# One-bank row tiles for the two seven-row output units of a soft-MoE kernel

## The chip, the cores and the metric

The kernel runs on one core of one Trainium2 chip. The metric is the device time of one execution in microseconds, the median of several runs. Lower is better.

## The reference

Four sequences of 5056 tokens with 256 channels go through a gated recurrence. The result goes, as one list of 20224 tokens, through a mixture of 8 experts with 4 slots each. Cut to what matters:

```python
h = f[:, t] * h + i[:, t] * x[:, t]          # recurrence over t; y[:, t] = h
logits = x @ phi                             # x is now y, as 20224 x 256; phi 256 x 32
d = exp(logits - logits.max(0)); d /= d.sum(0)
slot_input = d.T @ x                         # 32 x 256
slot_out = relu(slot_input[e] @ w1[e]) @ w2[e]   # 4 slots of each expert e
c = exp(logits - logits.max(1)); c /= c.sum(1)
out = c @ slot_out                           # 20224 x 256, float32, 20.7 MB
```

Only the last line is touched by the change: each token's output is a weighted sum of 32 slot rows, divided by the sum of its weights.

## The kernel before

Up to about 143 us the kernel runs the recurrence, the logits and the experts. It keeps three things for the end. `etall` holds exp(logits) as [slot, token], with the 32 slots of batch b on partitions 32b to 32b+31. `rrow` holds the reciprocal of each token's sum of weights. `slot_out` holds the slots' outputs on 128 partitions, a copy for each batch, and `slot_bd` (line 685, written by POOL) is the same in a block form, two batches side by side: with the weights of two batches on 64 partitions, one matmul against `slot_bd` gives 512 columns, 256 of each batch.

The 5056 tokens of a batch are cut into `blocks`: two of 2048 tokens (16 rows of 128), a last one of 896 (7 rows), and 64 tokens left over. A row is 128 tokens, one on each partition; within a block a partition holds consecutive tokens, so that a transfer writes 16 KB (or 7 KB) in one piece. The output stage works through units, in this order, written out by hand:

1. `pieces(0, 0)` (line 712): block 0 of batch 0 in nine small pieces, a matmul for each row, so that the first transfers can start early. Its PSUM tiles come from `pfirst`, eight buffers of one bank.
2. `couple(2, 0)` and `couple(2, 1)` (line 742): the seven-row block for batches 0 and 1, then for batches 2 and 3. Each tile of `pout` has two banks and takes two rows of two batches, so a unit has four tiles, the last with one row.
3. `rest()` (line 768): the 64 left-over tokens of all batches.
4. `whole(0, 1)` (line 731): block 0 of batch 1, four rows to a tile.
5. `couple(0, 1)`, `couple(1, 0)`, `couple(1, 1)`: sixteen rows of two batches each, eight tiles.

In every unit PE writes a PSUM tile, and DVE and ACT take the tiles in turn: they multiply by `rrow` into an SBUF tile (`ob` or `oc` of the pool `osb`, three buffers each). When a unit is complete, SP issues its transfers to HBM: 7 for `pieces`, two for each couple (one a batch), two for `rest`, one for `whole`, 20 in all. They go through one queue in the order of issue. Order on each engine is that of the program (a manual schedule).

A PSUM tile is reused when its reader has finished. A pool that opens where another one lay waits for all of the earlier pool's tiles: `pfirst` and `pout` both cover all eight banks, and `pout` opens behind `pieces`. Later tiles of `pout` wait only for the one whose buffer they take: `rest` for a tile of `couple(2, 1)` that DVE reads, `whole`'s first for one that ACT reads.

```python
with tc.tile_pool(name="pfirst", bufs=8, space=PSUM) as pfirst:
    pieces(0, 0)

pout = ctx.enter_context(tc.tile_pool(name="pout", bufs=4, space=PSUM))
```

Of the kernel before, what the change touches and what calls it, by code (L numbers as in the profile page):

```python
# [9 lines left out]
F32 = mybir.dt.float32  # L10
# [3 lines left out]
ACT = mybir.ActivationFunctionType  # L14
# [4 lines left out]
def kernel(  # L19
# [10 lines left out]
    nc = tc.nc  # L30
    B, S, D = x.shape
    E = moe_w1.shape[0]
    F = moe_w1.shape[2]
    NS = moe_phi.shape[1]
    SPE = NS // E
    P = 128
# [25 lines left out]
    blocks = [(i * P * wide_r, wide_r) for i in range(n_blk)]  # L62
# [57 lines left out]
    etall = store.tile([P, S + PAD], BF16, name="etall")[:, :S]  # L120
    rrow = store.tile([P, n_grp * R, B], F32, name="rrow")
# [6 lines left out]
    slot_bd = store.tile([P, 2, D], BF16, name="slot_bd")  # L128
# [33 lines left out]
    with tc.tile_pool(name="sp2", bufs=3) as sp2, \  # L162
# [316 lines left out]
        for n in range(n_unit):  # L479
# [14 lines left out]
            else:  # L494
                end = n >= n_unit - 6
# [94 lines left out]
        for o in range(DC):  # L590
            nc.tensor.matmul(sin_ps[:, o], slot_v[:, o], rep[:, 0],
                             start=True, stop=True, skip_group_check=True)
        spin(slot_bank[:, 1], 6, D)

    with tc.tile_pool(name="ew", bufs=1) as ew, \
# [16 lines left out]
        for q in range(E // Q):  # L612
            hi = ew.tile([P, F], BF16, name=f"hi{q}")
            for k in range(2):
                hi_ps = (psu.tile([P, H], F32, name="hi_ps", tag="up") if q == 0 else
                         pbig.tile([P, H], F32, name="hi_ps", tag=f"hi_ps{k}"))
                for o in range(DC):
                    for j in range(Q):
                        nc.tensor.matmul(hi_ps[ds(j * NS, NS)], sin[:, o],
                                         w1_sb[q * Q + j][:, o, ds(k * H, H)],  # L620
                                         start=(o == 0), stop=(o == DC - 1),
                                         skip_group_check=True)
# [30 lines left out]
        for e in range(Q):  # L653
            for fc in range(FC):
                nc.tensor.matmul(so4_ps[ds(fc % 4 * NS, NS), :], hid[:, fc, e],
                                 w2_sb[e][:, fc],
                                 start=(e == 0 and fc < 4),
                                 stop=(e == Q - 1 and fc >= FC - 4),
                                 skip_group_check=True)
# [7 lines left out]
        for j in range(Q):  # L667
            for fc in range(FC):
                nc.tensor.matmul(so_ps, wide[:, fc, j].rearrange("p b s -> p (b s)"),
                                 w2_sb[Q + j][:, fc], start=j == 0 and fc == 0,  # L670
                                 stop=j == Q - 1 and fc == FC - 1, skip_group_check=True)
            if j == 0:
                nc.tensor.matmul(so_ps, rep2, so4, start=False, stop=False,
                                 skip_group_check=True)
# [14 lines left out]
    with tc.tile_pool(name="osb", bufs=3) as osb:  # L689

        def by_vector(ob, op, scale):
            nc.vector.tensor_tensor(ob, op, scale.broadcast_to(list(ob.shape)), ALU.mult)  # L692
# [5 lines left out]
        def share(op, i, b, r, k):  # L698
            t0, n_r = blocks[i]
            ew = etall[ds(b * NS, NS), ds(t0, P * n_r)].rearrange("s (p r) -> s p r", r=n_r)  # L700
            for j in range(k):
                nc.tensor.matmul(op[:, j], ew[:, :, r + j], slot_out[ds(b * NS, NS)],  # L702
                                 start=True, stop=True, skip_group_check=True)

        def scale_of(i, b, r, k):
            return rrow[:, ds(blocks[i][0] // P + r, k), ds(b, 1)]

        def rows_of(i, b):
            t0, n_r = blocks[i]
            return out[ds(b * S + t0, P * n_r)].rearrange("(p r) d -> p r d", r=n_r)  # L710

        def pieces(i, b):
            dst = rows_of(i, b)
            obs = [osb.tile([P, blocks[i][1], D], F32, name="ob", tag="ob") for _ in range(2)]
            for j, r, k, ready in ((0, 0, 1, 1), (1, 1, 1, 1), (0, 2, 2, 2), (1, 4, 2, 2),
                                   (0, 6, 2, 2), (1, 8, 2, 0), (0, 12, 2, 0), (1, 10, 2, 4),
                                   (0, 14, 2, 4)):
                op = pfirst.tile([P, 2, D], F32, name="op", tag="op")
                share(op, i, b, r, k)
                (by_vector, by_scalar)[j](obs[j][:, ds(r, k)], op[:, ds(0, k)],  # L720
                                          scale_of(i, b, r, k))
                if ready:
                    q = ds(r + k - ready, ready)
                    nc.sync.dma_start(out=dst[:, q], in_=obs[j][:, q])

        with tc.tile_pool(name="pfirst", bufs=8, space=PSUM) as pfirst:
            pieces(0, 0)

        pout = ctx.enter_context(tc.tile_pool(name="pout", bufs=4, space=PSUM))

# [11 lines left out]
        def couple(i, j):  # L742
            t0, n_r = blocks[i]
            ew = etall[ds(j * 2 * NS, 2 * NS), ds(t0, P * n_r)].rearrange(
                "s (p r) -> s p r", r=n_r)
            scale = rrow[:, ds(t0 // P, n_r), ds(2 * j, 2)]
            ob = osb.tile([P, 2, n_r, D], F32, name="oc", tag="oc")
            for t, r in enumerate(range(0, n_r, 2)):
                k = min(2, n_r - r)
                op = pout.tile([P, 2, 2, D], F32, name="op", tag="op")  # L750
                for i_r in range(k):
                    nc.tensor.matmul(op[:, i_r].rearrange("p u d -> p (u d)"),  # L752
                                     ew[:, :, r + i_r],
                                     slot_bd[ds(j * 2 * NS, 2 * NS)].rearrange("s u d -> s (u d)"),
                                     start=True, stop=True, skip_group_check=True)
                if t % 2 == 0:
                    nc.vector.tensor_tensor(  # L757
                        ob[:, :, ds(r, k)].rearrange("p u r d -> p r u d"), op[:, ds(0, k)],
                        scale[:, ds(r, k)].unsqueeze(3).broadcast_to([P, k, 2, D]), ALU.mult)
                else:  # L760
                    for i_r in range(k):
                        for u in range(2):
                            nc.scalar.activation(ob[:, u, r + i_r], op[:, i_r, u], ACT.Copy,  # L763
                                                 scale=scale[:, r + i_r, ds(u, 1)])
            for u in range(2):
                nc.sync.dma_start(out=rows_of(i, 2 * j + u), in_=ob[:, u])

        def rest():
            n_p = B // 2
            op = pout.tile([P, n_p, 2, D], F32, name="op", tag="op")  # L770
            ob = osb.tile([P, n_p, D], F32, name="ob", tag="ob")
            for j in range(n_p):
                k = ds(j * 2 * NS, 2 * NS)
                nc.tensor.matmul(op[:, j].rearrange("p u d -> p (u d)"),
                                 left[k].rearrange("s t u -> s (t u)"),
                                 slot_bd[k].rearrange("s u d -> s (u d)"),
                                 start=True, stop=True, skip_group_check=True)
            nc.scalar.copy(ob, op[:, :, 0])
            nc.vector.tensor_tensor(ob, ob, op[:, :, 1], ALU.add)
            by_vector(ob, ob, rrow[:, n_grp * R - 1, ds(0, n_p)].unsqueeze(2))  # L780
            dst = out.rearrange("(b t) d -> t b d", b=B)
            for j in range(n_p):
                nc.sync.dma_start(out=dst[ds(S - L, L), ds(2 * j, 2)], in_=ob[:, j])

        end = len(blocks) - 1
        couple(end, 0)
        couple(end, 1)
        rest()
        whole(0, 1)
        for i in range(end):  # L790
# [33 lines left out]
```

## Time and profile before

| what | value |
|---|---|
| three runs | 198.64, 199.23, 199.25 us; median 199.23 |
| the profiled execution | 198.84 us, span 197.1 us |
| busy over the span | PE 77%, DVE 72%, ACT 70%, POOL 52% |
| HBM read, written | 58.23 MB, 20.71 MB |
| first output transfer issued | 144.10 us |
| couple(2, 0), couple(2, 1) issued from | 150.59 and 153.29 us |
| rest, whole(0, 1) issued from | 155.39 and 158.01 us |
| couple(0, 1), (1, 0), (1, 1) issued from | 164.72, 170.80 and 176.87 us |
| SP's last wait, for the output transfers | 17.1 us |

Times within the profile are counted from the start of the span. Busy shares are averages over stages with different limits, so the table says little about the end; the stretches and the timeline from 143 us on do. A busy PE is not PE at its peak, and its clock is granted in steps, which the page shows in tenths. In a timeline line the first number is the start, the second how long the group took, then engine, line, operation, out<-in, shapes and count, and in brackets the idle time before and who ended it. "PEld" is the loading of weights into PE, "SPq" an instruction that SP issues.

### The profile page before, as it was taken

The numbers are of one execution on the slowest core, as the hardware profiler recorded it, in microseconds if no ns is written. First come the engines' busy times: TensorE is split into PE (matmuls) and PEld (weight loads), VectorE is DVE, ScalarE is ACT, GpSimd is POOL, SyncE is SP. The second block draws the span as 40 slices with busy tenths as digits, with TensorE's granted clock in tenths as the row PEclk, the third lists the DMA queues.
The fourth block names the chain that finished last, engine by engine and source line by source line (L and its number), as shares of the span: only waits on it lengthen the run. The fifth ranks groups of instructions, "written<-read, shape, count | busy, mean of one in ns | idle before, by whom it ended". The sixth has DMA issues, their size and how long they took to land.

```text
span 197.1 us, 3226 instructions
## 1 busy us (share of the span) xinstructions
PE 151.9 (77%) x1195; PEld 106.4 (54%) x1195; DVE 142.1 (72%) x163; ACT 138.1 (70%) x193; POOL 103.1 (52%) x78
## 2 busy tenths in 40 slices
PE   0688598897999979897998888999769999960000
PEld 0477478675766758665776676668543643310000
DVE  2669769989799999999999999342268878850000
ACT  3588678799799998899997797240057889990000
POOL 2589578874998588894969977291030000000000
PEclk9999879999999999999999999999985555555555
DMA  5999999999999999999999999999658999999995
GB/s 201 418 420 423 428 431 421 426 427 358 378 429 421 392 353 426 421 412 308 408 419 381 254 220 215 213 214 213 122 197 352 429 429 432 449 429 426 426 426 216
DMA packets 14161, 70.75 MB, mean 359 GB/s; under 512 B 1585, under 2 KB 2866, under 8 KB 10178
## 3 DMA queue, kind: packets, MB, share of 16 engines
q1 hardware_dynamic: 11520, 62.13, 76.1%
q0 software_dynamic: 2624, 8.42, 21.4%
q8 instruction: 9, 0.15, 0.3%
q14 instruction: 6, 0.05, 0.1%
q10 hardware_dynamic: 2, 0.00, 0.0%
HBM read 58.23 MB, written 20.71 MB: 401 GB/s over the span
## 4 chain that ended last, share of the span: by engine, by line
DMA 29%; PE 27%; DVE 17%; POOL 7%; ACT 5%; issue 4%; ACTq 0%; SPq 0%; DVEq 0%; POOLq 0%
DMA x_t<-in_x_dram 14%; DVE h L313 12%; PE op L752 12%; DMA w_sb<-in_moe_w_dram 7%; DMA w_t<-in_moe_w_dram 7%; POOL u_t L246 6%; PE hp L326 3%; PE up L267 3%; DVE ht L345 3%; PE sp L261 2%; PE op L702 2%; PE slot_ps L183 1%; PE lg L359 1%; DVE ob L692 1%; ACT oc L763 1%
## 5 line engine op out<-in xcount | busy, mean ns | idle before, releaser
L246 POOL TENSOR_TENSOR u_t<-s_t,x_t 128x1024 bf16<-128x1024 bf16 (+1 forms) x39 | 82.4, 2129 | 22.1 <-ACT s_t L235 14.3
L313 DVE TENSOR_TENSOR_SCAN h<-a,h,up 128x512 bf16<-128x512 f32 (+1 forms) x72 | 86.8, 1252 | 4.4 <-PE up L267 1.7
L235 ACT ACTIVATE s_t<-f_t 128x2048 bf16<-128x2048 f32 (+2 forms) x23 | 38.3, 1668 | 6.4 <-DMA f_t<-in_f_logit_dram 6.0
L326 PE MATMUL hp<-ident_f,h 128*128 128x128 f32 (+1 forms) x160 | 29.5, 309 | 8.0 <-DVE ht L345 6.0
L326 PEld LDWEIGHTS hp<-ident_f,h 128*128 128x128 f32 (+1 forms) x160 | 23.2, 207 | 19.0 <-DVE ht L345 12.6
L261 PE MATMUL sp<-ident_f,s_t 128*128 128x128 f32 x144 | 22.3, 300 | 6.4 <-ACT s_t L235 4.5
L752 PE MATMUL op<-slot_bd,etall 64*128 64x512 bf16 x62 | 25.0, 621 | 1.6 <-DVE ob L692 1.4
L295 ACT ACTIVATE a<-sp,lbs 128x1024 f32<-128x1024 bf16 x24 | 25.4, 1115 | 0.6 <-PE sp L261 0.6
L763 ACT ACTIVATE oc<-op,rrow 128x256 f32<-128x256 f32 x60 | 22.7, 488 | 3.6 <-PE op L752 3.0
L757 DVE TENSOR_TENSOR oc<-op,rrow 128x1024 f32<-128x1024 f32 x16 | 19.3, 1222 | 6.0 <-PE op L752 6.0
L261 PEld LDWEIGHTS sp<-ident_f,s_t 128*128 128x128 f32 x144 | 18.0, 155 | 8.4 <-ACT s_t L235 5.4
L302 ACT ACTIVATE a<-sp,lbs 128x512 f32<-128x512 bf16 (+2 forms) x22 | 17.8, 858 | 4.7 <-PE sp L261 4.3
L267 PE MATMUL up<-ident_f,u_t 64*128 64x64 f32 x192 | 17.8, 230 | 2.2 <-POOL u_t L246 2.1
L752 PEld LDWEIGHTS <-etall 64*128 64x128 bf16 x62 | 9.0, 155 | 16.1 <-issue 12.5
L267 PEld LDWEIGHTS up<-ident_f,u_t 64*128 64x128 f32 x192 | 14.0, 138 | 6.2 <-POOL u_t L246 2.8
L183 PE MATMUL slot_ps<-rep,ident_f 128*128 128x256 f32 x52 | 16.7, 417 | 0.0
L345 ACT COPY ht<-hp 128x512 f32<-128x512 f32 (+1 forms) x20 | 11.6, 582 | 3.8 <-PE hp L326 3.7
L345 DVE COPY ht<-hp 128x512 f32<-128x512 f32 (+1 forms) x20 | 13.3, 666 | 0.8 <-PE hp L326 0.8
L696 ACT ACTIVATE ob<-op,rrow 128x256 f32<-128x256 f32 x15 | 5.8, 477 | 11.2 <-PE op L702 11.1
L313 DVE TENSOR_TENSOR_SCAN h<-a,up 128x512 bf16<-128x512 f32 x8 | 9.3, 1208 | 2.6 <-ACT a L302 1.7
L261 PE MATMUL up<-ident_f,u_t 128*128 128x128 f32 x48 | 9.5, 328 | 0.7 <-POOL u_t L246 0.7
L359 PE MATMUL lg<-h,phi 128*32 128x512 bf16 (+1 forms) x80 | 9.4, 389 | 0.3 <-ACT et L383 0.2
(110 smaller groups left out, 147.9 us busy)
## 6 DMA issues: line engine op xcount, KB each, us to landing
f_t<-in_f_logit_dram SPq DMA_DIRECT2D x12, 1024.0 KB, 12.3
x_t<-in_x_dram SPq DMA_DIRECT2D x12, 1024.0 KB, 11.9
out_dram<-oc SPq DMA_DIRECT2D x6, 2048.0 KB, 11.1
w_sb<-in_moe_w_dram POOLq DMA_DIRECT2D x14, 512.0 KB, 10.9
f_t<-in_f_logit_dram SPq DMA_DIRECT2D x12, 512.0 KB, 8.5
x_t<-in_x_dram SPq DMA_DIRECT2D x12, 512.0 KB, 9.9
out_dram<-oc SPq DMA_DIRECT2D x4, 896.0 KB, 5.2
out_dram<-ob SPq DMA_DIRECT2D x1, 2048.0 KB, 8.3
```

The costliest lines, as they stand in the source:

```text
L183: nc.tensor.matmul(slot_bank[:, 1], ident_f, wide_rep, start=False, stop=False, skip_group_check=True)
L235: nc.scalar.activation(s_t, f_t, ACT.Sigmoid, scale=-1.0)
L246: nc.gpsimd.tensor_tensor(uts[n][:, :r], s_t[:, :r], x_t[:, :r], ALU.mult)
L261: nc.tensor.transpose(ps[:, :, r], t[:, r], ident_f)
L267: nc.tensor.transpose(v[:, :, r], t(r)[k].bitcast(F32), ident_f[k, k])
L295: nc.scalar.activation(a, sp[:, :, :, :, o], ACT.Identity, scale=nomlb[:, ds(o, 1)], bias=1.0)
L313: nc.vector.tensor_tensor_scan(h[:, :T, o], decays[n // 2, o][:, n % 2, :T], up[:, :T, o], hs[number(g - 1, b)][:, ds(used(g - 1) - 1, 1), ...
L326: nc.tensor.transpose(hp[:n_p, r], hw[:, :n_p, r], ident_f)
L345: copy(hts[g][:n_p, b].rearrange("p r d -> p (r d)").bitcast(F32), hps.pop(n)[:n_p].rearrange("p r c -> p (r c)"))
L752: nc.tensor.matmul(op[:, i_r].rearrange("p u d -> p (u d)"), ew[:, :, r + i_r], slot_bd[ds(j * 2 * NS, 2 * NS)].rearrange("s u d -> s (u d)"),
L757: nc.vector.tensor_tensor(ob[:, :, ds(r, k)].rearrange("p u r d -> p r u d"), op[:, ds(0, k)], scale[:, ds(r, k)].unsqueeze(3).broadcast_t ...
L763: nc.scalar.activation(ob[:, u, r + i_r], op[:, i_r, u], ACT.Copy, scale=scale[:, r + i_r, ds(u, 1)])
```

## The change

The two seven-row units leave `couple` and get a function of their own, `by_rows`. It takes one tile of one bank for each row, with both batches in it (512 columns), from `pfirst`, in turn with the pieces' tiles. Even rows (four of seven) are evicted by DVE in one instruction of 512 columns; odd rows (three) by ACT in two of 256, one a batch. Matmuls, their order, the SBUF tile and the two transfers stay as they were. `pout` opens behind `by_rows`, so its first user is now `rest`.

```diff
+        def by_rows(i, j):
+            t0, n_r = blocks[i]
+            k = ds(j * 2 * NS, 2 * NS)
+            ew = etall[k, ds(t0, P * n_r)].rearrange("s (p r) -> s p r", r=n_r)
+            scale = rrow[:, ds(t0 // P, n_r), ds(2 * j, 2)]
+            ob = osb.tile([P, 2, n_r, D], F32, name="oc", tag="oc")
+            for r in range(n_r):
+                op = pfirst.tile([P, 2, D], F32, name="op", tag="op")
+                nc.tensor.matmul(op.rearrange("p u d -> p (u d)"), ew[:, :, r],
+                                 slot_bd[k].rearrange("s u d -> s (u d)"),
+                                 start=True, stop=True, skip_group_check=True)
+                if r % 2 == 0:
+                    by_vector(ob[:, :, r], op, scale[:, r].unsqueeze(2))
+                else:
+                    for u in range(2):
+                        nc.scalar.activation(ob[:, u, r], op[:, u], ACT.Copy,
+                                             scale=scale[:, r, ds(u, 1)])
+            for u in range(2):
+                nc.sync.dma_start(out=rows_of(i, 2 * j + u), in_=ob[:, u])
+
+        end = len(blocks) - 1
         with tc.tile_pool(name="pfirst", bufs=8, space=PSUM) as pfirst:
             pieces(0, 0)
+            by_rows(end, 0)
+            by_rows(end, 1)
 
         pout = ctx.enter_context(tc.tile_pool(name="pout", bufs=4, space=PSUM))
...
-        end = len(blocks) - 1
-        couple(end, 0)
-        couple(end, 1)
         rest()
         whole(0, 1)
```

On the engines' queues the number of matmuls, weight loads, activations and transfers is unchanged. DVE has eight instructions of 512 columns in place of four of 1024 (the last of each four with 512). In the second unit each row waits for the eviction of a row of the first unit, and the first matmul of `rest` waits for the last evictions of DVE and of ACT; `whole`'s first three tiles carry no wait of their own any more.

## The prediction

> **What bounds the kernel now.** I read the slices of the page first, then the stretches of the output stage with their transfer rates, then the timeline there, then the issues and landings. The slices (40 of 4.93 us) say who works last:
>
> ```profile
> PE   0688598897999979897998888999769999960000
> ...
> ACT  3588678799799998899997797240057889990000
> ...
> PEclk9999879999999999999999999999985555555555
> DMA  5999999999999999999999999999658999999995
> ```
>
> From about 152 us on DMA is at 9 and goes on for four slices after PE and ACT have stopped. So the end is set by output transfers. They run in one queue, in order of issue, and the stretches (columns: busy us and instruction count of PE, PEld, DVE, ACT, POOL; granted clock; DMA share; GB/s) show where that queue was not fed:
>
> ```profile
> 143.00:146.10 3.10, 1.97 (x16) 1.74 (x16) 2.62 (x6) 2.45 (x7) 1.83 (x2) 1.00 0.29 95
> 146.10:150.50 4.40, 3.81 (x11) 1.36 (x12) 2.70 (x4) 2.25 (x7) 0.00 (x0) 0.50 1.04 416
> 150.50:151.50 1.00, 1.00 (x4) 0.51 (x4) 1.00 (x2) 0.63 (x2) 0.00 (x0) 0.50 0.20 80
> 151.50:156.30 4.80, 4.80 (x21) 2.63 (x17) 3.69 (x5) 3.98 (x11) 0.00 (x0) 0.50 1.01 423
> 156.30:165.60 9.30, 9.30 (x25) 3.62 (x25) 7.56 (x8) 8.38 (x22) 0.00 (x0) 0.50 1.01 423
> ```
>
> There is one hole once the stream runs: in 150.5 to 151.5 the share is 0.20, so 0.8 us are lost. The timeline has its cause:
>
> ```profile
> 143.12 1.97 PE L702 MATMUL op<-slot_out,etall 32*128 32x256 bf16 x16
> 143.25 1.83 POOL L685 TENSOR_SCALAR slot_bd<-slot_out,parity 128x256 bf16<-128x256 bf16 x2 [9.64 <-DVE slot_out L683]
> 143.55 2.81 DVE L692 TENSOR_TENSOR ob<-op,rrow 128x256 f32<-128x256 f32 x5 [0.48 <-PE op L702]
> 143.65 2.68 ACT L696 ACTIVATE ob<-op,rrow 128x256 f32<-128x256 f32 x7 [10.28 <-PE op L702]
> ...
> 146.51 3.41 PE L752 MATMUL op<-slot_bd,etall 64*128 64x512 bf16 x9 [1.42 <-DVE ob L692]
> ...
> 147.63 1.22 DVE L757 TENSOR_TENSOR oc<-op,rrow 128x1024 f32<-128x1024 f32 x1 [1.27 <-PE op L752]
> ...
> 150.59 4.30 SPq L766 DMA_DIRECT2D out_dram<-oc  x4
> ```
>
> PE finishes the pieces at 145.09 and stands for 1.42 us until DVE (146.36) and ACT (146.33) have evicted the last of them: the two-bank pool lies on the banks of the first. DVE then stands 1.27 us for its first tile. So the first seven-row unit is issued at 150.59, when the pieces' bytes have just run out (150.5); its first bytes move some 0.84 us after the issue.
>
> A second margin matters as much. Ahead of couple(0, 1) the queue carries 2.10 MB of pieces, 3.67 of the seven-row units, 0.26 of the rest and 2.10 of whole(0, 1): 8.13 MB. Adding rate times length over the five stretches gives 8.17 MB by 165.6, so the queue runs dry there. couple(0, 1) is issued at 164.72, and with the same 0.84 its bytes start at 165.56. It arrives just in time. A hole filled earlier only pays if this issue moves too. It hangs on PE:
>
> ```profile
> 151.69 0.58 PE L774 MATMUL op<-slot_bd,left 64*128 64x512 bf16 x1
> ...
> 152.76 3.61 PE L702 MATMUL op<-slot_out,etall 32*128 32x256 bf16 x16
> ...
> 156.32 19.28 PE L752 MATMUL op<-slot_bd,etall 64*128 64x512 bf16 x48
> ...
> 164.72 13.79 SPq L766 DMA_DIRECT2D out_dram<-oc  x6
> ```
>
> From whole's first matmul (152.76) to that issue it is 11.96 us of dense PE work.
>
> **The change, part by part.**
>
> *Removed: the pool boundary ahead of unit 0.* Its rows take the eight one-bank buffers in turn. The first seven follow pieces that were evicted between 144.1 and 146.33, each before PE comes to its row. What is left is slot_bd: 143.25 + 1.83 = 145.08, plus 0.05 for a semaphore (slot_out's end at 143.07 to PE at 143.12). PE's first row starts at 145.13 and not at 146.51.
>
> *Replaced: eviction by row.* DVE had two 1024-wide tiles a unit, 1.22 each; now four 512-wide rows. The trace's mean for that shape is 0.68; two of them back to back take 1.28, so they follow at 0.60. Eight rows are 4.8 us against 4 x 1.14 = 4.6 (two 1024-wide in 2.36: 1.14 apart): 0.2 us more DVE work, hidden behind the stream; if the cover goes, 0.2 is its price. ACT keeps its 12 activations at about 0.36. PE keeps 14 matmuls.
>
> [...]
>
> *Unit 0's transfers.* DVE's rows start right behind the pieces, at 146.28; the fourth ends at 146.28 + 3 x 0.60 + 0.68 = 148.76. Before, issue followed DVE's end by 0.08; so 148.84, first bytes 149.7, before the pieces run out at 150.5. The hole of 0.8 us closes.
>
> *Unit 1.* If DVE paces, its last row ends at 146.28 + 7 x 0.60 + 0.68 = 151.16. If PE paces at the granted 0.50 from the start, rows are 0.43 apart (1.86 for four, the last one longer; 48 in 19.28): unit 0's seventh starts at 147.7, unit 1's first almost beside it (it uses the other 64 partitions, as L774 at 151.69 lies 0.07 from the L752 at 151.76), its seventh at 150.3, result 0.63 later, eviction 0.68 and a semaphore: 151.65.
>
> *Added: the boundary now lies ahead of rest.* Its first matmul (L774, 151.69 before) must wait for all fourteen rows: 151.2 to 151.7. Queued behind it on PE are rest's second matmul, whole's sixteen and all 48 of the couples, and on these hang DVE, ACT and SP. But whole no longer waits by itself. Before, it waited until 152.71 for an ACT tile of unit 1 (activations from 151.14); now it follows rest's first matmul by 0.43: 151.6 to 152.1, earlier by 1.1 to 0.6. ACT and DVE reach rest earlier too (ACT was busy to 153.3 with unit 1).
>
> *The transfers moved.* All twenty keep order, size and queue. The first six of unit and rest are issued 0 to 1.8 us earlier, behind a longer backlog, which costs SP time but starves nothing.
>
> *The sum.* The queue before couple(0, 1) runs dry at 165.6 - 0.8 = 164.8. couple(0, 1) is issued at 164.72 - 1.1 to 164.72 - 0.6, its bytes can start at 164.4 to 164.95. So the gain is 0.8 at one end and 0.65 at the other. I take 0.75, nearer DVE's pace, since the first PE rows still run at clock 1.00 (it falls near 146.1). All later transfers (12.6 MB) follow without a gap. The profiled execution took 198.84 (span 197.1 and 1.7 around it): 198.1. The median of the runs, 199.23, lies 0.4 above it: **198.5**.
>
> *The clock.* PE stood idle for about 1 us when the clock fell, and then 19 us of dense 64-partition matmuls did not bring it back. [...]
>
> **The rivals.**
>
> *The hole is smaller in other executions (chance 0.30).* Where the clock falls later than 146.1, PE in the kernel before does unit 0's rows 0.22 apart instead of 0.43 (the pieces' own matmuls were 0.12 apart at 1.00 and whole's 0.22 at 0.50), and unit 0 is issued 0.5 us or more earlier by itself. For it: three runs of the same kernel spread by 0.6 us (198.64 to 199.25), nearly the hole. Against it: two of three lie at the top. The gain is then 0.1 to 0.5: about 198.9.
>
> *The wait ahead of rest takes over (0.13, slower).* The place is rest's first matmul, behind the slowest of fourteen evictions. whole starts later than 152.76 if the last row ends after 152.3, that is if DVE's eight rows take over (152.3 - 146.36) / 8 = 0.74 each. For it: a lone 512-wide row takes 0.68 to 0.69, and two dependent ones on DVE were 0.72 apart. Against it: 0.60 in the pieces, the same operation from the same tiles. Beyond that point every delay is paid in full at couple(0, 1); at 0.80 a row, 0.5 us: 199.7.
>
> *It does not do what it says (0.07).* If PE cannot start before 146 (slot_bd later than POOL's rough span says, or a buffer held), unit 0 gets out at about 150 and rest starts at about 152.5: hole smaller by half, couple(0, 1) no earlier: 199.2. Against it: before, PE's wait named the last evictions, not POOL.
>
> **How the numbers follow.** The forecast has 0.50. About 0.3% (0.6 us) is what a measurement of this kernel can tell from no change; so faster means below 198.63, and the forecast's own range, 198.3 to 198.6, lies just beyond it. The first and third rival are no change, 0.37; the second is slower, 0.13. The range reaches down to 197.9, the lowest run before less 0.75, and up to 199.5, into the slower case.
>
> **What would show it.** Right: PE's first row near 145.1; unit 0 issued near 148.8; no stretch under a share of 0.9 after 146.5; rest's first matmul by 151.7, whole by 152.1; couple(0, 1) issued before 164.1. Wrong: DVE's rows 0.74 or more apart; a new hole where whole(0, 1) ends, near 164.7; or unit 0 issued before 150 in another execution of the old kernel.

## The result

| kernel | median, us | lowest to highest | runs |
|---|---|---|---|
| before | 198.64 | 197.78 to 199.53 | 17 |
| changed | 197.94 | 197.76 to 198.15 | 17 |

The ratio is 0.9968, with a 95% interval of 0.9953 to 0.9983: 0.64 us less, between 0.34 and 0.93. The profiled executions took 198.84 and 198.15 us. Two things stand out. The gain is there, small and clear of noise; and the changed kernel spreads over 0.4 us where the kernel before spreads over 1.75 (a later set of twelve runs of the changed kernel spread further, see "Half of the change"). Their lowest times are the same.

The stretches of the changed kernel's output stage (columns as before: busy us and counts of the five engines, granted clock, DMA share, GB/s):

```profile
146.10:150.50 4.40, 2.99 (x10) 0.98 (x8) 4.40 (x9) 4.40 (x13) 0.00 (x0) 0.71 1.03 409
150.50:151.50 1.00, 0.36 (x2) 0.11 (x2) 0.58 (x1) 0.15 (x1) 0.00 (x0) 0.50 1.06 442
151.50:156.30 4.80, 4.80 (x21) 2.96 (x20) 3.64 (x4) 3.11 (x8) 0.00 (x0) 0.50 1.02 426
156.30:165.60 9.30, 9.30 (x25) 3.46 (x23) 7.25 (x6) 8.50 (x23) 0.00 (x0) 0.50 1.05 440
```

The hole is gone: the share in 150.5 to 151.5 went from 0.20 to 1.06, and no other of these stretches lost anything. DVE and ACT are busy for all of 146.1 to 150.5, where each stood idle before. The timeline of the same kernel:

```profile
145.06 1.69 PE L734 MATMUL op<-slot_bd,etall 64*128 64x512 bf16 x8
146.12 4.52 ACT L741 ACTIVATE oc<-op,rrow 128x256 f32<-128x256 f32 x12
146.22 4.86 DVE L692 TENSOR_TENSOR oc<-op,rrow 128x512 f32<-128x512 f32 x8
147.05 2.48 PE L734 MATMUL op<-slot_bd,etall 64*128 64x512 bf16 x6 [0.30 <-ACT oc L741]
...
148.77 4.00 SPq L744 DMA_DIRECT2D out_dram<-oc  x4
...
151.14 0.60 PE L797 MATMUL op<-slot_bd,left 64*128 64x512 bf16 x2 [1.61 <-DVE oc L692]
...
151.68 3.63 PE L702 MATMUL op<-slot_out,etall 32*128 32x256 bf16 x16
...
155.26 19.30 PE L775 MATMUL op<-slot_bd,etall 64*128 64x512 bf16 x48
...
163.66 13.79 SPq L789 DMA_DIRECT2D out_dram<-oc  x6
```

PE goes from the pieces to the rows without a stop; eight DVE rows take 4.86 us in one run; the first unit is issued at 148.77 and couple(0, 1) at 163.66, 1.8 and 1.1 us earlier than before. PE now waits 1.61 us ahead of rest, until DVE's last row is done; it does no harm, since rest and couple(0, 1) still come earlier than before.

### The profile page after: what moved, and what is told of

Its sections match the earlier page's. It is cut to its first block, busy times and chain, and to the rows that moved or that the text cites. A ratio compares the mean times of both kernels' runs of the same rounds, so it can differ in the third digit from the quotient of the medians.

```text
span 196.4 us, 3226 instructions
## 1 busy us (share of the span) xinstructions
PE 151.1 (77%) x1195; PEld 106.5 (54%) x1195; DVE 142.3 (72%) x167; ACT 138.4 (70%) x193; POOL 103.2 (53%) x78
## 4 chain that ended last, share of the span: by engine, by line
PE 34%; DMA 23%; DVE 18%; POOL 7%; issue 4%; ACT 2%; ACTq 0%; DVEq 0%; POOLq 0%
DVE h L313 11%; PE op L775 10%; DMA w_sb<-in_moe_w_dram 7%; DMA w_t<-in_moe_w_dram 7%; DMA x_t<-in_x_dram 7%; POOL u_t L246 6%; PE hp L326 5%; PE sp L261 5%; PE up L267 4%; DVE ht L345 3%; DVE oc L692 2%; PE slot_ps L183 2%; PE lg L359 2%; DMA f_t<-in_f_logit_dram 2%; PE op L702 2%
## 5 line engine op out<-in xcount | busy, mean ns | idle before, releaser
L775 PE MATMUL op<-slot_bd,etall 64*128 64x512 bf16 x48 | 19.3, 621 | 0.0
L786 ACT ACTIVATE oc<-op,rrow 128x256 f32<-128x256 f32 x48 | 18.2, 492 | 1.1 <-PE op L775 0.5
L780 DVE TENSOR_TENSOR oc<-op,rrow 128x1024 f32<-128x1024 f32 x12 | 14.5, 1223 | 4.3 <-PE op L775 4.3
L183 PE MATMUL slot_ps<-rep,ident_f 128*128 128x256 f32 x52 | 17.5, 432 | 0.0
L775 PEld LDWEIGHTS <-etall 64*128 64x128 bf16 x48 | 7.2, 158 | 11.6 <-issue 10.3
```

What stands on the lines that cost most here:

```text
L183: nc.tensor.matmul(slot_bank[:, 1], ident_f, wide_rep, start=False, stop=False, skip_group_check=True)
L775: nc.tensor.matmul(op[:, i_r].rearrange("p u d -> p (u d)"), ew[:, :, r + i_r], slot_bd[ds(j * 2 * NS, 2 * NS)].rearrange("s u d -> s (u d)"),
```

## The experiments

Times of experiments stand beside runs of the kernel before on the same chip, with medians of 198.72 to 198.82. Places in the output stage are also given from PE's first matmul of the pieces, since that starts at 143.0 to 143.3 us in nearly every execution. "Lost" is the idle time of the 16 DMA engines once the stream was running, averaged over the engines, from the packet records of the trace; it is good to about 0.05 us.

### The kernel before, profiled again

> The kernel before, unchanged, profiled once more. Theory (the granted clock sets the hole): where the clock falls within 0.5 us of 146.1 counted as before, the first seven-row unit is issued near 150.6 and the stream has a hole of about 0.8 us; where it falls after 147.5, that unit is issued at 149.6 to 150.0, the hole is 0.3 us or less and the time is 0.5 us or more lower. Rival (the spread of the times comes from the load stage, ahead of 143 us): the stage from 143 us to the end takes the same 52 us in every execution, and the difference lies before it.

> As for the first look: the same kernel in another execution. Theory: the length from the first matmul of the pieces to the last transfer goes with the time at which the clock falls, 0.8 us between an early and a late fall. Rival: that length is the same, and the start of the output stage moves.

| execution | clock falls, from first matmul | first seven-row unit issued | lost | time, us |
|---|---|---|---|---|
| before, the profile shown | 3.0 | 7.47 | 0.85 | 198.84 |
| before, second profile | 4.9 | 6.53 | 0.18 | 197.98 |
| before, third profile | 4.8 | 6.52 | 0.14 | 198.15 |
| changed | 4.9 | 5.71 | 0 | 198.15 |

From the second profile, two stretches and the timeline:

```profile
146.10:150.40 4.30, 3.65 (x12) 1.65 (x14) 3.45 (x4) 2.55 (x7) 0.00 (x0) 0.72 1.04 417
150.40:150.90 0.50, 0.50 (x3) 0.15 (x1) 0.38 (x1) 0.49 (x2) 0.00 (x0) 0.50 1.06 438
```

```profile
146.53 1.76 PE L752 MATMUL op<-slot_bd,etall 64*128 64x512 bf16 x7 [1.42 <-DVE ob L692]
147.23 3.55 DVE L757 TENSOR_TENSOR oc<-op,rrow 128x1024 f32<-128x1024 f32 x3 [0.85 <-PE op L752]
...
149.67 0.81 SPq L766 DMA_DIRECT2D out_dram<-oc  x2
```

PE waits the same 1.42 us at the boundary. But at full clock seven matmuls take 1.76 us, DVE waits 0.85 and not 1.27, and the unit is issued at 149.67, before the pieces' bytes run out. So the same kernel loses 0.85 us or some 0.15, by where the clock falls; of the 0.15 a part is lost at the first seven-row unit and a part ahead of couple(0, 1), near 164.7 us. The three start the pieces at 143.12 to 143.29 us, so the stage before them does not make this difference. The changed kernel's profile takes as long as the third although it lost nothing: its stream began worse, with a share of 0.53 in the microsecond from 145.3 us against 0.77 in the second profile, before the stretch that "lost" counts. In the three profiles of before the clock falls 3.0, 4.9 and 4.8 us after the same matmul; what sets that moment was not shown.

### PE kept busy at the boundary

```diff
             pieces(0, 0)
+            kept = pfirst.tile([P, 2, D], F32, name="kept", tag="op")
+            for _ in range(5):
+                nc.tensor.matmul(kept.rearrange("p u d -> p (u d)"), ident, etall[:, ds(0, 2 * D)],
+                                 start=True, stop=True, skip_group_check=True)
```

> The kernel before, with five full-array matmuls (128 partitions, 512 columns, 1.1 us at full clock) on PE between the pieces and the pool boundary; nothing reads what they write, the output is the same. Theory (the hole depends on the clock): PE stays at clock 1.00 until 148 us or later in most executions, the first unit's rows come 0.22 apart, it is issued at 149.6 to 150.0, the hole shrinks to 0.3 us or less: 0.3 to 0.7 us faster than the kernel before in the median, and the spread of its times shrinks to under 0.8 us. Rival (the boundary alone makes the hole): no change in the median, 198.4 to 198.9, same spread of 1.7 us.

Measured: 197.98 (197.85 to 198.12, 12 runs) against 198.76 (197.86 to 199.09): ratio 0.9969, 0.9956 to 0.9981. Its timeline:

```profile
145.00 1.25 PE L730 MATMUL kept<-etall,ident 128*128 128x512 bf16 x5
146.49 1.69 PE L756 MATMUL op<-slot_bd,etall 64*128 64x512 bf16 x7 [0.24 <-DVE ob L692]
...
149.63 0.84 SPq L770 DMA_DIRECT2D out_dram<-oc  x2
```

```profile
146.10:150.50 4.40, 3.69 (x14) 1.62 (x15) 3.55 (x4) 2.79 (x8) 0.00 (x0) 0.87 1.04 415
150.50:151.50 1.00, 1.00 (x5) 0.21 (x2) 0.61 (x2) 1.00 (x4) 0.00 (x0) 0.50 1.08 450
```

The boundary, the two-row tiles and the order are those of the kernel before, yet the time and the spread are those of the changed one. The clock fell 6.25 us after the first matmul, and nothing was lost. So in these runs the hole needs two things at once: the wait at the boundary (1.42 us) and a clock that falls early, by about the time the unit's first matmuls run (3.0 us after the first matmul, where 0.85 us were lost, against 4.8 and 4.9, where 0.14 and 0.18 were). Taking away either is worth the same, with ratios of 0.9968 and 0.9969. That the rows need no late fall is seen in two kernels further down that keep the change and have their fall 3.1 us after the first matmul (the one of "The second margin, by itself" and the one with 19 transfers and the pieces as they were): the first unit is issued after 5.72 us in both, as in the changed kernel's profile with its fall at 4.9.

### Rows, but behind the boundary

```diff
             pieces(0, 0)
+        with tc.tile_pool(name="prows", bufs=8, space=PSUM) as prows:
             by_rows(end, 0)
             by_rows(end, 1)
...
-                op = pfirst.tile([P, 2, D], F32, name="op", tag="op")
+                op = prows.tile([P, 2, D], F32, name="op", tag="op")
```

> The change with one part undone: the rows keep one bank and eviction by row, but their eight buffers are a pool of their own that opens behind the pieces, so the boundary is back ahead of the first unit. Theory (the gain is the removed wait at the boundary): PE starts the rows near 146.5 and not 145.1; with the clock at 0.50 the first unit is issued near 150.4 and whole starts 0.7 us later than in the kernel before; with the clock at 1.00 it is issued near 149.5. Median between 198.2 and 199.4, and the spread of the kernel before, over 1 us. Rival (eviction by row is the gain, by letting DVE start on half a tile): near the changed kernel, 197.9 to 198.1, with its small spread of 0.4 us.

Measured: 198.74 (198.06 to 199.18, 12 runs), ratio to before 1.0006, 0.9987 to 1.0024. One stretch and the timeline:

```profile
150.30:151.20 0.90, 0.16 (x1) 0.00 (x0) 0.90 (x2) 0.90 (x4) 0.00 (x0) 1.00 0.20 79
```

```profile
146.43 4.03 PE L734 MATMUL op<-slot_bd,etall 64*128 64x512 bf16 x14 [1.42 <-DVE ob L692]
146.99 0.69 DVE L692 TENSOR_TENSOR oc<-op,rrow 128x512 f32<-128x512 f32 x1 [0.71 <-PE op L734]
...
147.85 0.69 DVE L692 TENSOR_TENSOR oc<-op,rrow 128x512 f32<-128x512 f32 x1 [0.16 <-PE op L734]
...
150.32 3.99 SPq L744 DMA_DIRECT2D out_dram<-oc  x4
```

DVE's first row comes 0.6 us before the first two-row tile of the kernel before, and that gains nothing: at half clock PE paces the rows, DVE waits 0.16 before each, the unit goes out at 150.32 and the hole is back at a share of 0.20. whole starts 9.96 us after the first matmul, 0.3 later than in the kernel before and not 0.7 as expected: the clock came back for a while (last section). The gain of the change is the wait that it removes, not eviction by row.

### Half of the change

```diff
             by_rows(end, 0)
-            by_rows(end, 1)
...
+        couple(end, 1)
         rest()
```

> The changed kernel, unchanged, as the measure for the others here. Every theory: 197.8 to 198.2, spread under 0.5 us.

> Half of the change: the first seven-row unit by rows from the first pool, the second as two-row tiles from the two-bank pool, whose boundary now lies between the two units. Theory (two margins: the hole at 150.5 and the issue of couple(0, 1)): the hole closes (unit issued near 148.8), but PE stands until about 148.7 at the boundary, whole starts at about 152.4 and couple(0, 1) is issued at about 164.4, so its bytes start near 165.2 where the queue runs dry at 164.8: a new hole of 0.2 to 0.5 us; 0.2 to 0.5 us slower than the changed kernel. Rival (only the hole at 150.5 counts): the same time as the changed kernel.

Measured: changed kernel 198.01 (197.82 to 199.29, 12 runs), half of it 198.03 (197.90 to 198.56, 12 runs). The changed kernel's spread of 1.5 us is beyond the 0.5 expected of it. Its highest time is the profiled one, and there the first matmul of the pieces started 1.4 us late (144.49), while its output stage was as always; the other high times have no profile. In the profile of the half, the new hole is where it was expected:

```profile
148.69 2.76 PE L774 MATMUL op<-slot_bd,etall 64*128 64x512 bf16 x6 [1.09 <-DVE oc L692]
...
152.30 3.57 PE L702 MATMUL op<-slot_out,etall 32*128 32x256 bf16 x16
...
164.22 0.81 SPq L788 DMA_DIRECT2D out_dram<-oc  x2
```

```profile
164.00:164.50 0.50, 0.50 (x2) 0.16 (x1) 0.49 (x1) 0.50 (x3) 0.00 (x0) 0.50 0.61 262
164.50:165.00 0.50, 0.50 (x3) 0.15 (x2) 0.20 (x1) 0.50 (x3) 0.00 (x0) 0.50 0.02 0
```

The first unit is out at 148.7, PE stands 1.09 us at the boundary between the units, whole starts at 152.30 and couple(0, 1) is issued at 164.22, too late for the queue: 0.48 us are lost. The medians do not show it. They are equal, and four of 12 times of the half lie above 198.3, against three. The packet records say why it costs less than 0.48: all 16 engines stood still together for only 0.21 us of it, and the last byte of the stream landed 51.43 us after the first matmul, against 51.23 in the changed kernel's profile beside it. So the mechanism is seen, and a price of 0.2 us in this one execution, in which the clock fell early (after 2.6 us); the expected 0.2 to 0.5 us in the median is not.

### The second margin, by itself

```diff
-                share(op, i, b, r, k)
+                for _ in range(1 if r else 3):
+                    share(op, i, b, r, k)
```

> The changed kernel with the four matmuls of whole's first tile done three times, eight more of 256 columns, 1.7 us at clock 0.50; same values, same output. Theory (couple(0, 1) has a slack of about 0.3 us in the changed kernel): couple(0, 1) is issued 1.7 us later, near 165.3, a hole of 1.3 to 1.5 us opens where whole's bytes end, and the time is 1.3 to 1.5 us longer than the changed kernel's. Rival (the end is set by the amount of bytes alone once the queue is full): no change, under 0.2 us.

Measured: 199.11 (198.88 to 200.32, 12 runs), 1.1 us above the changed kernel beside it. A stretch and the timeline:

```profile
164.50:166.50 2.00, 2.00 (x6) 0.78 (x5) 1.70 (x3) 2.00 (x7) 0.00 (x0) 0.50 0.31 131
```

```profile
151.82 5.34 PE L702 MATMUL op<-slot_out,etall 32*128 32x256 bf16 x24
...
165.40 0.81 SPq L790 DMA_DIRECT2D out_dram<-oc  x2
```

A delay on PE of 1.7 us, 13 us ahead of the transfer that it holds up and with the queue full at that time, comes out at the end. Counted from the first matmul, couple(0, 1) is issued after 22.20 us, 1.60 later than in the changed kernel (20.60), and the packet records show all 16 engines at rest for 1.27 us: the slack was 0.3 us, as expected. The last byte lands after 52.42 us, 1.19 later than in the changed kernel's profile beside it (51.23); the medians differ by 1.1, a little under the expected 1.3 to 1.5. The amount of bytes alone does not set the end: couple(0, 1) must be issued in time.

### A version that gains more, and why

```diff
-            for j, r, k, ready in ((0, 0, 1, 1), (1, 1, 1, 1), (0, 2, 2, 2), (1, 4, 2, 2),
-                                   (0, 6, 2, 2), (1, 8, 2, 0), (0, 12, 2, 0), (1, 10, 2, 4),
-                                   (0, 14, 2, 4)):
+            for j, r, k, ready in ((0, 0, 2, 2), (1, 2, 2, 2), (0, 4, 2, 2), (1, 6, 2, 2),
+                                   (0, 8, 2, 0), (1, 12, 2, 0), (0, 10, 2, 4), (1, 14, 2, 4)):
```

> The changed kernel with the pieces cut into eight of two rows, where it had two of one row and seven of two; the first transfers then carry 2 KB from a partition, not 1 KB. Theory (the start of the stream is the next margin: the two 1 KB transfers take 0.7 us each for 0.13 MB, the 2 KB ones 0.65 for 0.26 MB): first bytes 0.25 us later, but the pieces are done 0.4 to 0.5 us earlier; DVE is done with the pieces 0.3 us earlier and couple(0, 1) is issued 0.2 to 0.3 us earlier; 0.2 to 0.5 us faster than the changed kernel. Rival (the first bytes count, and the stream's start is paced by the evictions): 0 to 0.25 us slower.

> The pieces in pairs, unchanged, as the measure for the kernel beside it. Every theory: 197.4 to 197.7; where the clock falls before 145.5 a hole of about 0.2 us stands where whole's bytes end, where it falls later none.

Measured: 197.54 (197.37 to 197.90, 7 runs) and 197.59 (197.34 to 197.71, 6 runs), 0.4 us below the changed kernel, as expected; but not for the reason given. The last byte of the stream lands 51.24 us after the first matmul in both profiles, and 51.23 in the changed kernel's on that chip. The stream gained nothing, and in the second of these profiles, with the clock falling at 147.1, about 0.1 us was lost where whole's bytes end, where none was expected. The next kernel still rests on that theory; it sends couple(0, 1) in halves, so that no hole can stand ahead of it:

```diff
+                if i == 0 and r in (6, 14):
+                    for u in range(2):
+                        nc.sync.dma_start(out=rows_of(i, 2 * j + u)[:, ds(r - 6, 8)],
+                                          in_=ob[:, u, ds(r - 6, 8)])
-            for u in range(2):
-                nc.sync.dma_start(out=rows_of(i, 2 * j + u), in_=ob[:, u])
+            if i:
+                for u in range(2):
+                    nc.sync.dma_start(out=rows_of(i, 2 * j + u), in_=ob[:, u])
```

> The changed kernel with the pieces in pairs, and couple(0, 1) sent in four transfers instead of two: rows 0 to 7 of both batches after its fourth tile, rows 8 to 15 at its end (8 KB from a partition). Theory (couple(0, 1)'s issue is the last margin left): its first transfer goes out some 3.4 us earlier, no hole is left after the pieces in any execution, and the time is 0.1 to 0.2 us below the pieces in pairs alone, 197.3 to 197.5, with a spread under 0.4 us. Rival (the smaller transfers cost as much as the hole): 0 to 0.3 us above the pieces in pairs alone.

Measured: 197.92 (197.83 to 198.10, 10 runs), 0.33 above the pairs alone, where 0.1 to 0.2 below had been expected. Nothing was lost in the stream, as expected, and the last byte landed after 51.32 us, hardly later. What differs lies behind the last byte. In the traces of before and of the changed kernel the 20 transfers use eight completion counters in turn, and SP ends the program by waiting for these eight, in the same order in both. From the trace's records, in us from the last byte:

```
changed, 20 transfers:  waits at 0.49 0.55 0.61 0.67 0.74 0.79 0.86 0.92; span ends at 1.80
halves, 21 transfers:   waits at      0.48 0.54 0.60 0.66 0.72 0.79 0.85; span ends at 1.75
pairs, 19 transfers:    wait  at                                    0.48; span ends at 1.37
```

With 20 transfers the last one uses the counter that is waited for first, and the seven others, long done, follow at 0.06 us each. With 19 it uses the last in the list. Two runs tell this from the pieces:

```diff
+            if j == 1:
+                two = out.rearrange("(b s) d -> b s d", b=B)[ds(2 * j, 2), ds(t0, P * n_r)]
+                nc.sync.dma_start(out=two.rearrange("b (p r) d -> p b r d", r=n_r), in_=ob)
+            else:
+                for u in range(2):
+                    nc.sync.dma_start(out=rows_of(i, 2 * j + u), in_=ob[:, u])
```

> The changed kernel with the two transfers of the second seven-row unit made one (both batches, 7 KB from a partition each): 19 output transfers instead of 20, pieces as they were. Theory (the end behind the last byte: SP waits for eight completion counters in a fixed order, 0.06 us each, and with 20 transfers the last one's counter stands first in that list, with 19 last): SP has one wait left after the last byte instead of eight, the span ends 1.4 us after the last byte instead of 1.8, and the time is 0.35 to 0.45 us below the changed kernel, 197.4 to 197.65; the stream itself is unchanged. Rival (the pieces in pairs gained by an earlier stream): no change, 197.9 to 198.1.

Measured: 197.45 (197.38 to 197.59, 6 runs), ratio to the kernel before 0.9935, 0.9910 to 0.9961. The pieces are untouched and the last byte lands after 51.28 us. And the pairs with one transfer more:

```diff
-                                   (0, 8, 2, 0), (1, 12, 2, 0), (0, 10, 2, 4), (1, 14, 2, 4)):
+                                   (0, 8, 2, 2), (1, 12, 2, 0), (0, 10, 2, 2), (1, 14, 2, 4)):
```

> The pieces in pairs with one transfer of four rows cut into two of two rows: 20 output transfers again. Theory (the count of transfers made the gain): the time goes back up by 0.35 to 0.45 us, to 197.85 to 198.1, with 1.8 us from the last byte to the end of the span. Rival (pairs of rows fill the stream's start better): it stays at 197.4 to 197.7.

Measured: 197.87 (197.77 to 198.12, 12 runs). The gain goes with the count, not with the pairs. The waits of SP show it too: what was waited for, us in total, times, longest. The changed kernel first, then the one with 19:

```profile
SPq L839 <- DMA out_dram<-oc: 17.5, 1, 17.5
```

```profile
SPq L843 <- DMA out_dram<-oc: 16.8, 4, 4.8
```

With 20 there is a single wait of 17.5 us, for the last transfer at once. With 19 SP works through the list while the earlier couples land, 4.8 us apart, and has one wait left at the end. This version, the change with the second unit's two transfers made one, has the lowest median measured: 0.5 us below the changed kernel's two (197.94 and 198.01), which were not taken beside it.

## Why the prediction was right

The mechanism held at each step. *PE's first row*: 145.13 foretold, 145.06 measured (2.01 and 2.00 us after the pieces' first matmul). *DVE's rows*: 0.60 apart foretold, eight in 4.86 us measured, which is 0.60 apart with 0.68 for the last, as the rows of the pieces had said. *Unit 0's issue*: 148.84 and 148.77. *rest's first matmul*: 151.2 to 151.7 and 151.14. *whole's*: 151.6 to 152.1 and 151.68. *couple(0, 1)'s issue*: 163.6 to 164.1 and 163.66. DVE paced unit 1, as chosen, with the clock at 1.00 until 147.9. The prediction had it fall near 146.1, and that difference is not what made these times come out: in the two kernels that keep the change and whose clock fell 3.1 us after the first matmul, near 146.2, whole started after the same 8.62 us as in the changed kernel's profile. The queue did not run dry again.

The gain was 0.75 in the sum; 0.69 between the two profiled executions, 0.70 between the medians, 0.64 by the ratio. That the two profiled executions come so close to the sum is in part chance: from the first matmul to the last byte the kernel before took 52.13 us and the changed one 51.52 there and 51.23 in its second profile, 0.6 or 0.9 less. The sum was for the hole of one execution, and its first rival said that in other executions the hole is smaller. Both were true, and one of the prediction's own signs of being wrong came: in the other two profiles of the kernel before the first seven-row unit was issued before 150 us, at 149.67 and 149.82. The kernel before has executions with 0.85 us lost and with 0.15, and seven of its 17 times are 198.2 or less; the changed kernel lost nothing in either of its profiles. The forecast held for the median because the larger part of the executions, ten of 17 above 198.2 us, are of the kind with the larger hole; had the rival's kind been the larger, the median would hardly have moved, by the same mechanism.

What was off is the term that set the sum on the median: 199.23 from three runs stood above the kernel's usual 198.64, so 198.5 came out 0.56 above the measured 197.94. That lies below the forecast's own range of 198.3 to 198.6 and only just inside the wide one, which reached down to 197.9. The spread of 0.6 us in three runs was read as a reason for a rival; it was also a reason to distrust their median, and the profiled 198.84 was the nearer of the two.

The slower rival, a wait ahead of rest that takes over, did not come: its point was 0.74 us a row, and rows came at 0.60. The delayed whole bears out what stood behind it: the changed kernel has 0.3 us of slack at couple(0, 1), where the sum for DVE's pace had 0.4 (164.8 against 164.4), and most of a delay beyond that reaches the end.

The paragraph on the clock was too quick. Dense 64-partition matmuls did not bring the clock back in the profile of before (the couples' 48, 19.28 us, ran at 0.50). Nor did the fall need a PE that stands: in the profile of the delayed whole the clock fell 3.10 us after the first matmul, and PE had been busy for 3.06 of these. But with five full-array matmuls in the gap it fell 6.25 us after the first matmul, later than in any profile of before, so in this kernel the clock was a part of the hole itself, not only of its range.

## What to carry to other kernels

Where a queue of transfers sets the end, look for every moment at which it runs dry, and for the next one that comes up when the first is closed; what is gained at the first is kept only as far as the second is ready in time. A wait of PE at a pool boundary can cost twice, by itself and by a clock that falls around it (here 1.42 us of wait lost the stream 0.85 us with the fall at 3.0 us and 0.14 to 0.18 with a later one), and a kernel whose times spread by far more than its neighbours' is worth a second profile before its parts are priced. At the very end, count the transfers: which counter the last one uses decided 0.4 us here, against 0.64 for the change.

## What the runs showed that was not expected

The end of the program: seven waits on counters that were long complete still took 0.43 us, 0.06 each, and merging two transfers into one took that away.

The clock in the kernel with rows behind the boundary: it fell 3.5 us after the first matmul and came back for 3.4 us, at 149.99 us, though only 64-partition matmuls had run. Those of the two units use different partitions, and in this profile they start in pairs, 0.01 us apart, from 147.6 us on; that this is the reason was not tried.
